# Layer-norm statistics and token sums at other products, a clamp on GpSimd and five denominators on ScalarE, in a linear-attention and ReGLU block

## The chip, the cores and the metric

The kernel runs on one core of one Trainium2 chip. The metric is the time of one execution in microseconds (us); lower is better. Next to each time stands the span, from the first instruction to the last in the core's own records.

The engines: PE is TensorE, DVE VectorE, ACT ScalarE, POOL GpSimd, SP the engine that issues most DMAs.

## The reference

```python
def A(x, wqkv, wo):                        # S = 2048, D = 1024, 32 heads of 32
    q, k, v = split(x @ wqkv)
    phi = lambda t: where(t > 0, t + 1, exp(t)) + 1e-6
    kv, z = sum_s phi(k) v, sum_s phi(k)   # linear attention, not causal
    o = (phi(q) @ kv) / (phi(q) . z + 1e-6)
    return o @ wo
h  = x + A(layernorm(x), wqkv, wo)
h2 = h + ReGLU_FFN(layernorm(h))           # F = 3584; gate * (gate > 0) * up, then W_down
```

## The kernel before

Large products are not done block by block. A *group* forms a 2 by 2 block product from seven smaller products, P1 to P7, of four matmuls each (a fast matrix multiplication). DVE forms sums of the tokens (`x_sums`) and of the weights beforehand; ACT copies PSUM banks between the products (the *fork copies* `fk1`, `fk2`, and `s7`, `sc`), since a later product accumulates on a copy of an earlier one. Other work is hung between the products: `hook(i)` runs its own functions, and those that the group before left in `pend[i]`.

```python
def sgroup(...):                                       # cut to the order of things
    prod(a, X(0,0), W(0,0), True, "P1");  ident_act(bank(b), bank(a), ...)  # fk1, ACT
    hook(1)
    prod(f, SX(2), TW(2), True, "P7");    ident_act(s7, bank(f), ...)
    hook(2)
    prod(b, SX(1), TW(1), False, "P6");   ident_act(bank(c), bank(b), ...)  # fk2, ACT
    hook(3)
    prod(a, X(1,0), W(1,0), False, "P2")  # then e11
    hook(4)
    prod(c, SX(0), TW(0), False, "P5");   ident_act(sc, bank(c), ...)
    hook(5)
    prod(b, X(1,1), TW(3), False, "P4")
    hook(6)
    prod(c, SX(3), W(1,1), False, "P3")
    pend[1] = list(s22[2:]) + s12 + list(s21[1:])      # phi's of this group, in the next
    hook(7)
```

The function phi is an exponential on ACT (`ex`), then on DVE a clamp and a max (`fin`):

```python
def fin():
    PL.add("dve", lambda e: e.tensor_scalar(out=E, in0=E, scalar1=1.0, scalar2=1e-6,
                                            op0=ALU.min, op1=ALU.add), ...)          # clamp
    PL.add("dve", lambda e: e.scalar_tensor_tensor(out=dst_ap, in0=src, scalar=C1, in1=E,
                                                   op0=ALU.add, op1=ALU.max), ...)   # max
```

The order of the work: start-up; groups k0, v2, k1, v3, k2, v4, k3, v5, k4, v6, k5, v7, k6, k7 (kN and vN form the keys and the values of pair N of token tiles, 2N and 2N+1; "P6 of k1" is product P6 of group k1); four query groups for the first half of the tokens and four for the second half; an output stage of 16 token tiles; the FFN. For the token tiles 7, 9, 11, 13 and 15 the first layernorm's statistics are three steps on ACT (a mean, and two halves of the squares, "split"; tiles 5 and 6 have their squares in one piece, the other tiles' statistics are on DVE), then come small operations on GpSimd, and a normalisation on DVE (`norm`). Their results live in slots, `k = len(ln1_a) % 2`.

```python
def v2(sq=sq):                  # hooks of a v group; sq holds tile 7's squares (p == 0), else nothing
    if sq: sq.pop(0)()          # first half of them, behind P7
def v3(p=p, sq=sq):
    if sq: sq.pop(0)()          # second half, behind P6
    if p == 0: x_sums(1); norm(6)
    else: norm(2 * p + 6)
def v5(p=p):
    norm(2 * p + 7)
    m_, q0_, q_ = ln1_stats_act(2 * p + 9, True)
    m_(); q0_(); late_q.append(q_)       # q_ runs at hook 5 of the next k group
...
def a2_div(st):                 # o = num / den, in the second half of the query groups and later
    # dtmp: DVE adds 1e-6 to the denominators (PSUM, 128x32); rden: DVE reciprocal; o: DVE product
    dma_t(..., oT, o, "T3d_%d" % st)     # DMA transpose of o, issued on SP
for t in range(4, 21):          # output stage; NOT = 4
    if t >= 4: a4_mm(t - 4)              # needs the transposed o of that tile
    if t < 16: a2_num(t); a2_div(t)
    if t >= 4: a4_h(t - 4)               # h = x + product (DVE); frees the product's two banks
    if t >= 5: a4_norm(t - 5)            # ACT, then a DMA transpose of the normalised h, on SP (T5d)
```

The instructions of DVE run in the order of the program, and SP issues its DMAs in order (traces in e5 and e6).

## Time and profile before

| | before |
|---|---|
| time, 4 runs beside the change | 723.83 us (723.75 to 724.64) |
| span of the profiled run | 722.1 us, clock 0.999 |
| PE / DVE / ACT / POOL busy | 714.2 / 587.5 / 359.2 / 108.4 us |

The page of the kernel before, its line of busy times:

```profile
PE 714.2 (99%) x4905; PEld 380.4 (53%) x4905; DVE 587.5 (81%) x1024; ACT 359.2 (50%) x623; POOL 108.4 (15%) x177
```

PE looks full, but a busy PE is not a PE that starts matmuls as fast as it can; the Trainium skill says that the busy share of matmuls is no good measure of the distance to the limit ("Perfetto Trace Analysis", Identifying the Most-Contended Engine), and here the fastest kernel at the end of this study and one of the slowest (e15, 723.9 us of span) both show 99%. What can be won is where the start times break their spacing of 0.86 to 0.88 us per product. PE's waits of the kernel before, from 0 to 240 us (after that there is none); the columns are the wait in total, how often, the longest:

```profile
PE ps L766 <- POOL RXH L545: 1.4, 1, 1.4
PE ps L905 <- DVE RXH L834: 1.1, 1, 1.1
PE ps L766 <- DVE RXH L1229: 0.7, 1, 0.7
PE ps L766 <- ACT ps L771: 0.5, 1, 0.5
PE ps L766 <- DVE RWG L984: 0.4, 1, 0.4
```

The first two lie before 7 us, at the start of the program. The last three are the change's targets. Their places in PE's timeline of the kernel before (start, length, engine, line, operation; in brackets the idle time before it and what ended that):

```profile
31.69 1.02 PE L766 MATMUL ps<-RW,RWG 128*128 128x512 f16 x4 [0.41 <-DVE RWG L984]
32.55 1.03 PE L766 MATMUL ps<-RAB 128*128 128x512 bf16 x4
33.63 1.04 PE L766 MATMUL ps<-RW,RWG 128*128 128x512 f16 x4
...
37.84 1.03 PE L766 MATMUL ps<-RC,RWG 128*128 128x512 f16 x4
39.39 1.04 PE L766 MATMUL ps<-RC,RWG 128*128 128x512 f16 x4 [0.53 <-ACT ps L771]
...
175.79 2.98 PE L766 MATMUL ps<-RW,RE 128*128 128x512 bf16 x13 [0.70 <-DVE RXH L1229]
```

31.69 is P6 of v2, which waits for the token sums (L984) and starts 0.57 later than the spacing would have it; 33.63 is its P5, 1.08 after P2 (32.55), so 0.22 late, though no wait is marked; 39.39 is P6 of k1, 1.55 after P7, so 0.69 late, waiting for a fork copy. ACT's timeline shows why that copy was late:

```profile
36.95 1.06 ACT L804 ACTIVATE RXH<-RE 128x1024 bf16<-128x1024 bf16 x1 [1.58 <-DVE RXH L890]
...
38.13 0.63 ACT L804 ACTIVATE RXH<-RE 128x512 bf16<-128x512 bf16 x1
...
38.76 0.58 ACT L771 ACTIVATE ps<-ps 128x512 f32<-128x512 f32 x1
```

ACT stood idle for 1.58 us before the mean of tile 9 (36.95), until the normalisation of tile 6 (L890) had read its slot of statistics; the mean and half of the squares then ran into the time of the fork copy (38.76).

### The profile page before, as it was taken

What the parts mean: (1) busy time and instruction counts of PE and PEld (TensorE: products, weight loads), DVE (VectorE), ACT (ScalarE), POOL (GpSimd) and SP (SyncE); (2) the same over time, 40 slices, a digit from 0 to 9 for tenths busy, and PEclk for the clock granted to TensorE, in tenths of its full rate; (3) what the DMA queues carried; (4) which work ended last, traced back from release to release, by engine and by line L of the source; (5) the groups of instructions that cost most, each with busy time, mean ns of one, the idle gap of its engine ahead of it and who ended that gap; (6) DMA issues with size and microseconds to landing.
All of it is one profiled execution on the core that took longest, in us unless ns stands there. A gap on an engine that the chain in (4) does not pass through costs nothing.

```text
span 722.1 us, 12877 instructions
## 1 busy us (share of the span) xinstructions
PE 714.2 (99%) x4905; PEld 380.4 (53%) x4905; DVE 587.5 (81%) x1024; ACT 359.2 (50%) x623; POOL 108.4 (15%) x177
## 2 busy tenths in 40 slices
PE   8999999999999999999999999999999999999998
PEld 3444444444444444444444558865555545447887
DVE  7878867898775889889988787887889877887984
ACT  4877666764842456677756111035455545423010
POOL 2311100000360103332321001310000000000331
PEclk9999999999999999999999999999999999999999
DMA  9643245023998797999999989993564572037996
GB/s 310 214 98 80 44 126 163 6 30 72 211 221 262 230 282 236 273 302 312 298 273 275 310 251 322 319 208 114 149 172 135 161 250 78 1 102 249 323 315 178
DMA packets 192989, 143.64 MB, mean 199 GB/s; under 512 B 51872, under 2 KB 170400, under 8 KB 192928
## 3 DMA queue, kind: packets, MB, share of 16 engines
q1 hardware_dynamic: 188224, 138.50, 65.3%
q0 software_dynamic: 4032, 3.67, 3.5%
q8 instruction: 38, 0.62, 0.3%
q10 hardware_dynamic: 672, 0.66, 0.3%
q14 instruction: 23, 0.19, 0.1%
HBM read 98.76 MB, written 32.51 MB: 182 GB/s over the span
## 4 chain that ended last, share of the span: by engine, by line
PE 90%; DVE 6%; issue 1%; ACT 1%; POOL 1%; DMA 0%; ACTq 0%; DVEq 0%
PE ps L766 90%; DVE RAB L852 1%; DVE RE L1205 1%; DVE st L780 1%; DVE RX L849 1%; POOL rstd L790 0%; DVE RW L959 0%; DMA RE<-in_A_x_dram 0%; DVE RC L959 0%; DVE RX L1065 0%; ACT RX L845 0%; ACT RXH L804 0%; DVE RXH L834 0%; DVE rden L1203 0%; ACT ps L771 0%
## 5 line engine op out<-in xcount | busy, mean ns | idle before, releaser
L771 ACT ACTIVATE ps<-ps 128x512 f32<-128x512 f32 (+1 forms) x192 | 108.8, 567 | 217.4 <-PE ps L766 207.1
L766 PE MATMUL ps<-RC,RO 128*128 128x512 f16 x616 | 143.0, 369 | 0.0
L766 PE MATMUL ps<-RH,RWG 128*128 128x512 bf16 x448 | 108.1, 379 | 0.0
L766 PEld LDWEIGHTS ps<-RC,RO 128*128 128x128 f16 x616 | 60.3, 98 | 63.5
L766 PE MATMUL ps<-RC,RWG 128*128 128x512 f16 x320 | 76.7, 379 | 0.5 <-ACT ps L771 0.5
L766 PEld LDWEIGHTS ps<-RH,RWG 128*128 128x128 bf16 x448 | 43.8, 98 | 46.9
L1447 DVE TENSOR_TENSOR RAB<-ps,RAB 128x512 bf16<-128x512 f32 x56 | 37.3, 686 | 31.3 <-PE ps L766 31.3
L766 PE MATMUL ps<-RH,RO 128*128 128x512 bf16 (+1 forms) x256 | 61.2, 379 | 0.0
L766 PE MATMUL ps<-RW,RE 128*128 128x512 bf16 x256 | 57.6, 380 | 0.7 <-DVE RXH L1229 0.7
L1647 POOL DMA_DIRECT2D out_dram<-RX x20 | 17.9, 1257 | 263.3 <-DVE RX L1638 221.0
L766 PE MATMUL ps<-RAB 128*128 128x512 bf16 (+2 forms) x270 | 57.1, 351 | 0.1
L766 PE MATMUL ps<-RW,RAB 128*128 128x256 f16 (+3 forms) x362 | 52.9, 301 | 0.0
L766 PEld LDWEIGHTS ps<-RC,RWG 128*128 128x128 bf16 (+1 forms) x320 | 30.1, 98 | 40.1 <-ACT ps L771 6.1
L771 ACT ACTIVATE RE<-ps 128x512 f32<-128x512 f32 (+1 forms) x64 | 31.5, 502 | 37.8 <-PE ps L766 37.8
L766 PEld LDWEIGHTS ps<-RW,RAB 128*128 128x128 f16 (+1 forms) x362 | 35.4, 98 | 14.5
L1638 DVE TENSOR_TENSOR RE<-ps,RE 128x512 f32<-128x512 f32 x44 | 30.2, 687 | 14.3 <-PE ps L766 13.8
L771 ACT ACTIVATE RAB<-ps 128x512 bf16<-128x512 f32 x56 | 33.3, 595 | 16.5 <-PE ps L766 16.2
L1331 DVE TENSOR_TENSOR RO<-RWG 128x1024 f16<-128x1024 bf16 x54 | 36.9, 684 | 4.9 <-DMA RWG<-in_B_W_up_dram 4.9
L766 PEld LDWEIGHTS ps<-RH,RO 128*128 128x128 f16 (+1 forms) x256 | 24.4, 98 | 29.9 <-ACT RX L771 1.5
L1442 ACT ACTIVATE RAB<-RAB 128x1024 bf16<-128x1024 bf16 x28 | 29.5, 1055 | 19.5 <-DVE RAB L1433 19.0
L766 PEld LDWEIGHTS ps<-RW,RE 128*128 128x128 bf16 x256 | 24.0, 98 | 28.7 <-DVE RXH L1229 1.2
L766 PEld LDWEIGHTS ps<-RAB 128*128 128x128 bf16 (+1 forms) x270 | 26.0, 98 | 24.4 <-ACT RAB L908 1.0
(163 smaller groups left out, 1169.6 us busy)
## 6 DMA issues: line engine op xcount, KB each, us to landing
RWG<-in_B_W_gate_dram SPq DMA_DIRECT2D x28, 512.0 KB, 6.2
RWG<-in_B_W_up_dram SPq DMA_DIRECT2D x28, 512.0 KB, 5.2
RW<-l_scr SPq DMA_DIRECT2D x20, 448.0 KB, 5.6
RW<-in_B_W_down_dram SPq DMA_DIRECT2D x14, 512.0 KB, 5.2
t_scr<-RW SPq DMA_DIRECT2D x14, 512.0 KB, 4.9
l_scr<-RX SPq DMA_DIRECT2D x7, 1024.0 KB, 6.5
RE<-l_scr SPq DMA_DIRECT2D x15, 448.0 KB, 4.9
RE<-in_A_x_dram SPq DMA_DIRECT2D x23, 256.0 KB, 3.8
```

Source lines behind the costliest of these rows:

```text
L766: lambda e: e.matmul(out_ap, lhsT, rhs, start=start, stop=stop, skip_group_check=skip),
L771: PL.add("act", lambda e: e.activation(out=dst, in_=src, func=func), reads=reads, writes=writes, name=name)
L780: PL.add("dve", lambda e: e.bn_stats(out=st6[:, k, c * 6:(c + 1) * 6], in_=src_full[:, c * BCH:(c + 1) * BCH]), reads=[src_chunk_bufs[c]], ...
L849: PL.add("dve", lambda e: e.tensor_scalar(out=Et[:, k, :], in0=Et[:, k, :], scalar1=1.0, scalar2=1e-6, op0=ALU.min, op1=ALU.add), reads=[] ...
L852: PL.add("dve", lambda e: e.scalar_tensor_tensor(out=dst_ap, in0=src, scalar=C1, in1=Et[:, k, :], op0=ALU.add, op1=ALU.max), reads=[src_bu ...
L1205: PL.add("dve", lambda e: e.tensor_tensor(out=osb[:, k, :].rearrange("p (g h e) -> p g h e", h=HPG, e=Dh), in0=nv[:, :, :, 0:Dh], in1=rden ...
L1331: PL.add(eng, lambda e: e.tensor_tensor(out=tb(j, u), in0=f0(u), in1=f1(u), op=ALU.subtract), reads=[B_w[i + x] for x in r] + ([B_T[k + x] ...
L1442: PL.add("act", lambda e: e.activation(out=d, in_=d, func=ACTF.Relu), reads=[], writes=db, name=name)
L1447: PL.add("dve", lambda e: e.tensor_tensor(out=d, in0=bank(b), in1=d, op=ALU.mult), reads=[B_bank[b]], writes=[db], name=name)
L1638: PL.add(eng, lambda e: e.tensor_tensor(out=dst, in0=in0, in1=in1, op=op), reads=reads, writes=writes, name=name)
L1647: PL.add("pool", lambda e: e.dma_start(dst, src, accum_op=ALU.add), reads=[bsrc], writes=[B_hscr[st]], slot=sl, name="acc_%d_%d" % (st, dh))
```

## The change

The intent is to take away these waits. (1) A third slot of statistics; tile 7's squares one product later; tile 9's squares both at hook 5 of k1; for tiles 11, 13 and 15 the first half of the squares two products earlier; one difference of weights for v moved from before k0 to k0's hook 6, and the third pair's token sums one hook earlier. (2) In the second half of the query groups one of four clamps runs on GpSimd, and its max one group later at `pend[3]`; the `dtmp` of tiles 0 to 4 runs on ACT. The diff, cut to its core:

```diff
-            k = len(ln1_a) % 2
+            k = len(ln1_a) % 3
@@ sgroup(..., late=False)
-            pend[1] = list(s22[2:]) + s12 + list(s21[1:])
+            tail = list(s21[1:])
+            if late:
+                pend[3] = [tail.pop()]
+            pend[1] = list(s22[2:]) + s12 + tail
@@ q group
-                   add_phi(*dst(1, 0), "q_%d_%d" % (r, ct)),
-                   add_phi(*dst(1, 1), "q_%d_%d" % (r, ct)), "q%d%d" % (r, ct), hooks)
+                   add_phi(*dst(1, 0), "q_%d_%d" % (r, ct), ("dve", "pool")[r]),   # clamp's engine
+                   add_phi(*dst(1, 1), "q_%d_%d" % (r, ct)), "q%d%d" % (r, ct), hooks, late=r == 1)
@@ a2_div
+            if st <= NE:
+                PL.add("act", lambda e: e.activation(out=dv, in_=nv[:, :, :, Dh], func=ACTF.Identity, bias=tiny[:]), ...)
+            else: ...                                  # on DVE, as before
@@ before k0
-        twv.pop(0)()                                   # a difference of weights, DVE 1.2 us
@@ hooks of the k groups
+            def k4():
+                if p == 0: x_sums(2, 0)
             def k5():
+                if p == 0: x_sums(2, 1)
...
+                while p > 0 and late_q: late_q.pop(0)()
             def k6():
+                if p == 0: twv.pop(0)()
@@ hooks of the v groups
-                v2: first squares half;  v3: second half;  p == 0: x_sums(1), norm(6)
+                v3: first squares half;  v4: second half;  p == 0: norm(6), x_sums(1)
-                v5: m_(); q0_(); late_q.append(q_)
+                v5, p == 0: m_(); late_q.extend([q0_, q_])
+                p > 0: q0_() already at v3, the mean at v5   # cut
```

More of the change, by code (lines that the diff above doesn't have):

```diff
@@ L341, in bass_sequential_preLN__linear_attn_block__glu_gated_reglu__prompt_kernel @@
         neghalf = sb("neghalf", [P, 1], f32)
+        tiny = sb("tiny", [P, 1], f32)
         warm = sb("warm", [P, 8], f32)
@@ L346, in bass_sequential_preLN__linear_attn_block__glu_gated_reglu__prompt_kernel @@
         s2 = sb("s2", [P, 2, 5], f32)
-        s1 = sb("s1", [P, 2, 4], f32)
+        s1 = sb("s1", [P, 3, 4], f32)
         dtmp = sb("dtmp", [P, NDT, H], f32)
@@ L427, in bass_sequential_preLN__linear_attn_block__glu_gated_reglu__prompt_kernel @@
         B_s2 = [bufs("s2_%d_" % i, 5) for i in range(2)]
-        B_s1 = [bufs("s1_%d_" % i, 4) for i in range(2)]
+        B_s1 = [bufs("s1_%d_" % i, 4) for i in range(3)]
         B_junk = _Buf("junk")
@@ L464, in bass_sequential_preLN__linear_attn_block__glu_gated_reglu__prompt_kernel @@
         B_neghalf = _Buf("neghalf")
+        B_tiny = _Buf("tiny")
         B_warm = _Buf("warm")
@@ L557, in bass_sequential_preLN__linear_attn_block__glu_gated_reglu__prompt_kernel @@
         PL.add("pool", lambda e: e.memset(warm[:], 0.0), writes=[B_warm], name="warm0")
+        PL.add("pool", lambda e: e.memset(tiny[:], 1e-6), writes=[B_tiny], name="tiny")
         def act_warm():
@@ L838, in bass_sequential_preLN__linear_attn_block__glu_gated_reglu__prompt_kernel, with phi_steps @@
         phi_ctr = [0]
-        def phi_steps(src, src_buf, dst_ap, dst_buf, name):
+        def phi_steps(src, src_buf, dst_ap, dst_buf, name, eng="dve"):
             k = phi_ctr[0] % NPH
@@ L846, in ex, with low, fin @@
                        reads=[src_buf], writes=[B_E[k]], name=name + "_exp")
-            def fin():
-                PL.add("dve", lambda e: e.tensor_scalar(out=Et[:, k, :], in0=Et[:, k, :], scalar1=1.0,
+            def low():
+                PL.add(eng, lambda e: e.tensor_scalar(out=Et[:, k, :], in0=Et[:, k, :], scalar1=1.0,
                                                       scalar2=1e-6, op0=ALU.min, op1=ALU.add),
                        reads=[], writes=[B_E[k]], name=name + "_e2")
+            def fin():
+                if eng == "dve":
+                    low()
                 PL.add("dve", lambda e: e.scalar_tensor_tensor(out=dst_ap, in0=src, scalar=C1, in1=Et[:, k, :],
@@ L854, in fin, with exlow @@
                        reads=[src_buf, B_E[k]], writes=[dst_buf], name=name + "_phi")
-            return ex, fin
+            if eng == "dve":
+                return ex, fin
+            def exlow():
+                ex()
+                low()
+            return exlow, fin
         def phi(*args):
@@ L993, in x_sums, with sgroup @@
             add(3, xb(1, 0), s(1), ALU.subtract, [B_Sx[1][p]] + bx(1, 0))
-        def sgroup(pool, tok_major, X, SX, W, TW, e11, e12, e21, e22, name, hooks=(), isphi=True):
+        def sgroup(pool, tok_major, X, SX, W, TW, e11, e12, e21, e22, name, hooks=(), isphi=True, late=False):
             hooks = dict(hooks)
@@ L1060, in flush, with add_phi @@
             pend.clear()
-        def add_phi(dst, dst_buf, name):
+        def add_phi(dst, dst_buf, name, eng="dve"):
             def go(p_, pb, s_, sb_):
@@ L1066, in add @@
                            writes=[sb_], name=name + "_add")
-                return (add,) + phi_steps(s_, sb_, dst, dst_buf, name)
+                return (add,) + phi_steps(s_, sb_, dst, dst_buf, name, eng)
             return go
@@ L1199, in a2_div @@
             nv = ps[:, 0:HPG, 0:NG * NUW].rearrange("p h (g w) -> p g h w", w=NUW)
-            PL.add("dve", lambda e: e.tensor_scalar(
-                out=dtmp[:, kd, :].rearrange("p (g h) -> p g h", h=HPG), in0=nv[:, :, :, Dh],
-                scalar1=1e-6, scalar2=None, op0=ALU.add), reads=rb, writes=[B_dt[kd]], name="dtmp_%d" % st)
+            dv = dtmp[:, kd, :].rearrange("p (g h) -> p g h", h=HPG)
+            if st <= NE:
+                PL.add("act", lambda e: e.activation(out=dv, in_=nv[:, :, :, Dh], func=ACTF.Identity, bias=tiny[:]),
+                       reads=rb + [B_tiny], writes=[B_dt[kd]], name="dtmp_%d" % st)
+            else:
+                PL.add("dve", lambda e: e.tensor_scalar(out=dv, in0=nv[:, :, :, Dh], scalar1=1e-6, scalar2=None,
+                                                        op0=ALU.add),
+                       reads=rb, writes=[B_dt[kd]], name="dtmp_%d" % st)
             PL.add("dve", lambda e: e.reciprocal(out=rden[:, kd, :], in_=dtmp[:, kd, :]),
@@ L1960, in k1 @@
                     twq.pop(0)()
+            def k4():
+                if p == 0:
+                    x_sums(2, 0)
             def k5():
-                if p + 2 < NP_:
+                if p == 0:
+                    x_sums(2, 1)
+                elif p + 2 < NP_:
                     x_sums(p + 2, 0)
@@ L1968, in k5 @@
                     sq.extend([q0_, q_])
-                elif B < NST:
+                while p > 0 and late_q:
                     late_q.pop(0)()
             def k6():
-                if p + 2 < NP_:
+                if p == 0:
+                    twv.pop(0)()
+                elif p + 2 < NP_:
                     x_sums(p + 2, 1)
-            return {1: k1, 5: k5, 6: k6}, sq
+            return {1: k1, 4: k4, 5: k5, 6: k6}, sq
         def norm(st):
@@ L1998, in bass_sequential_preLN__linear_attn_block__glu_gated_reglu__prompt_kernel, with v3 @@
             if p + 2 < NP_:
-                def v2(sq=sq):
-                    if sq:
-                        sq.pop(0)()
-                def v3(p=p, sq=sq):
+                late = []
+                def v3(p=p, sq=sq, late=late):
                     if sq:
@@ L2006, in v3, with v4, v5 @@
                     if p == 0:
+                        norm(6)
                         x_sums(1)
-                        norm(6)
                     else:
                         norm(2 * p + 6)
-                def v5(p=p):
+                        if 2 * p + 9 < NST:
+                            m_, q0_, q_ = ln1_stats_act(2 * p + 9, True)
+                            q0_()
+                            late += [m_, q_]
+                def v4(sq=sq):
+                    if sq:
+                        sq.pop(0)()
+                def v5(p=p, late=late):
                     norm(2 * p + 7)
-                    B = 2 * p + 9
-                    if B < NST:
-                        m_, q0_, q_ = ln1_stats_act(B, True)
-                        m_()
-                        q0_()
-                        late_q.append(q_)
+                    if p == 0:
+                        m_, q0_, q_ = ln1_stats_act(9, True)
+                        m_()
+                        late_q.extend([q0_, q_])
+                    elif late:
+                        late[0]()
+                        late_q.append(late[1])
                 def v6(p=p, nq=nq):
@@ L2024, in v6 @@
                         twq.pop(0)()
-                v_group(p + 2, {2: v2, 3: v3, 5: v5, 6: v6})
+                v_group(p + 2, {3: v3, 4: v4, 5: v5, 6: v6})
         assert not twq and not twv and not twk
```

## The prediction

> **What bounds the kernel.** TensorE: the page gives PE 714.2 of 722.1 us busy. Matmul busy time is a poor measure of the distance to the limit (the Trainium skill, "Perfetto Trace Analysis", Identifying the Most-Contended Engine), so I took the spacing of matmul starts from the timeline: a product of four 128x512 matmuls starts every 0.86 to 0.88 us nearly everywhere, at a granted clock of 1.00. Only breaks of this spacing can be won. PE's waits and the timeline show, after the start-up, which the change leaves alone:
> - 31.69 (first v group, P6): 0.57 us over the spacing, for DVE's token sums;
> - 33.63 (same group, P5): 0.22, ACT's second fork copy was late, behind a squares half;
> - 39.39 (second k group, P6): 0.69, ACT's first fork copy started at 38.76, its product had ended at 38.0; ACT was at statistics (mean 36.95, squares 38.13);
> - 175.79 (third output product): 0.77, its banks are freed by h_0 on DVE, busy without a pause since about 163.
> Sum 2.25 us, 0.3%. No such wait stands in later k/v groups or the rest of the query part; after 176 PE keeps its spacing.
>
> **What the change does.**
> 1. It moves one weight difference (DVE 1.22 us, at 27.07) from before the first k group's evictions to its hook 6, and pair 2's token sums one product earlier. The sums end about 1.2 us earlier: the 0.57 goes.
> 2. The squares come one product later, behind the second fork copy: the 0.22 goes.
> 3. A third statistics slot frees the mean of tile 9 from the normalisation of tile 6 (36.29 to 36.84, just before it); ACT was idle from 35.4. Its squares move to the next k group. The 0.69 goes. There two squares halves (0.61 each in ACT's spacing) now stand in one product; the next first fork copy had no slack (ended 45.48, P6 at 45.51), so I give back 0.1.
> 4. In the second half of the query groups, one of four clamps (DVE 0.28) goes to GpSimd, its max one group later, and five denominators (DVE 0.18 each) to ACT. DVE has about 6.7 us of work per 6.53 us group; with 0.5 less it keeps up. But denominator 3 now stands on ACT behind the last exponential, which waits for the last product (ended 167.46): the reciprocal can't start before about 168.4, as before (168.39). From there to h_0's end (7.27 us) only one clamp and denominator 4 leave: of the 0.77 about 0.5 goes.
> GpSimd does a two-input 128x512 in 1.15 us here; I estimate the one-input clamp at no more. Its reader has 1.7. GpSimd shares SBUF interfaces with VectorE (the Trainium skill, "GPSIMD Engine Reference", Specifications), which could lengthen some DVE operations by little.
>
> **Sum.** -0.57 -0.22 -0.69 +0.1 -0.5 = -1.9: 723.8 to 721.9 us, -0.26%. Range 721.1 to 723.3. Faster by over 2%: 0.5%; within 2%: 99%; slower: 0.5%.
>
> **What would show it.** PE's waits have no entries near 31, 33 and 38; near 44 perhaps one of 0.1; near 174, 0.2 to 0.3 remain. DVE busy falls by about 2 us, ACT rises by 1 to 1.5, POOL by about 4. The time from the fifth output product to the end is unchanged within 0.2.
>
> **What would make it wrong.** ACT too full in the second k group; the moved weight difference delays the phi operations and with them pair 1's sums, which the second k group needs (slack about 0.7 by my count); ACT's strided read of PSUM slower than 0.3; the clamp late, so that DVE stands in order behind it; start-up scatter of up to 0.9 us, as the runs before show (723.75 to 724.64), half of the effect.

## The result, and the profile after

| | before | after |
|---|---|---|
| time, 4 runs each of the same rounds | 723.83 us (723.75 to 724.64) | 724.31 us (723.42 to 724.74) |
| span of the profiled run | 722.1 us, clock 0.999 | 722.3 us, clock 1.0 |

The ratio is 1.0002, with a 95% interval of 0.9985 to 1.0020: the same. The predicted 721.9 is missed, and its range (721.1 to 723.3) does not hold the measured time.

The page after, busy times, and PE's waits from 0 to 240 us:

```profile
PE 711.7 (99%) x4849; PEld 380.4 (53%) x4905; DVE 585.6 (81%) x1015; ACT 359.1 (50%) x628; POOL 118.8 (16%) x182
```

```profile
PE ps L769 <- POOL RXH L547: 1.4, 1, 1.4
PE ps L769 <- issue: 1.1, 7, 0.2
PE ps L769 <- DVE RXH L1250: 0.6, 1, 0.6
PE ps L769 <- ACT ps L774: 0.5, 1, 0.5
PE ps L918 <- DVE RXH L837: 0.3, 1, 0.3
```

(56 matmul records are missing in the trace of after, 4849 against 4905; the weight loads are complete. Each hole reads as a wait for "issue", so those seven are no waits.) DVE fell by 1.9 us, as predicted. The two waits of the key and value groups are off the list; one for a fork copy (ACT ps) is new, at another place, and the wait for h_0 (0.7) has become 0.6, not 0.2 to 0.3. PE's timeline after, at the places shown of before:

```profile
30.82 2.02 PE L769 MATMUL ps<-RW,RWG 128*128 128x512 f16 x8
32.89 0.81 PE L769 MATMUL ps<-RAB 128*128 128x512 bf16 x3
33.65 1.04 PE L769 MATMUL ps<-RW,RWG 128*128 128x512 f16 x4
...
37.98 1.93 PE L769 MATMUL ps<-RC,RWG 128*128 128x512 f16 x8
...
175.97 2.76 PE L769 MATMUL ps<-RW,RE 128*128 128x512 bf16 x11 [0.59 <-DVE RXH L1250]
```

P7 and P6 of v2 are now one piece of eight matmuls, and so are those of k1: the waits are gone, as predicted. And yet P5 of v2 starts at 33.65, where it started at 33.63 before. The waits went, and PE arrived no earlier.

To see where the time goes I cut both traces at landmarks: starts of weight loads on PE (complete in all traces) and of fork copies on ACT. Two traces of the same kernel give the same lengths within 0.02 us for most pieces, so 0.1 us can be read here, which a total time does not allow. ("First transposes" are PE's first of the normalised tokens, at 6.66 us in the trace of before. The whole span is these pieces, plus 6.3 to 6.8 us before the first transposes, 9.9 in e17, plus 3.9 after the last weight load.)

| piece, us | before | after | difference |
|---|---|---|---|
| first transposes to P6 of k0 | 18.34 | 19.03 | +0.69 |
| P6 of k0 to P6 of v2 | 6.66 | 6.21 | -0.45 |
| P6 of v2 to its P5 | 1.97 | 1.85 | -0.12 |
| P5 of v2 to P6 of k1 | 5.76 | 5.22 | -0.54 |
| to fk2 of k1 | 1.08 | 1.14 | +0.06 |
| to fk2 of v7 | 58.30 | 58.55 | +0.25 |
| to fk1 of k6 | 5.09 | 5.37 | +0.28 |
| to fk2 of the 2nd query group, second half | 46.74 | 46.74 | 0.00 |
| to the output product of tile 1 | 20.55 | 20.77 | +0.22 |
| to that of tile 2 | 4.63 | 4.53 | -0.10 |
| tile 2 to 8; 8 to 10; 10 to the FFN | 23.18; 7.73; 19.91 | 23.18; 7.74; 19.91 | +0.01 |
| FFN to its last weight load | 491.57 | 491.56 | -0.01 |

So 1.11 us of waits are gone, 0.69 came in before them and 0.71 behind them (the time before the first transposes was 0.11 shorter after; together this is the 0.2 between the spans). Three questions follow. Is the +0.69 of the start-up the change's doing or scatter? What are +0.25 and +0.28? Why did the query part lose 0.22 and win only 0.10?

ACT's timeline gives the mechanism of the first. Before, and then after, the mean of tile 6 in the start-up:

```profile
20.43 1.07 ACT L804 ACTIVATE RXH<-RE 128x1024 bf16<-128x1024 bf16 x1
```

```profile
21.40 1.06 ACT L807 ACTIVATE RXH<-RE 128x1024 bf16<-128x1024 bf16 x1 [0.98 <-DMA RE<-in_A_x_dram]
```

After, ACT stood idle 0.98 us until the load of that tile had landed; everything behind the mean in ACT's order, k0's first fork copy too, came later. The change touches neither this load nor the order of ACT up to there.

### The profile page after: what moved, and what is told of

Read it like the earlier page. It is cut to its first block, busy times and chain, and to the rows that moved or that the text cites. A ratio compares the mean times of both kernels' runs of the same rounds, so it can differ in the third digit from the quotient of the medians.

```text
span 722.3 us, 12827 instructions
## 1 busy us (share of the span) xinstructions
PE 711.7 (99%) x4849; PEld 380.4 (53%) x4905; DVE 585.6 (81%) x1015; ACT 359.1 (50%) x628; POOL 118.8 (16%) x182
## 4 chain that ended last, share of the span: by engine, by line
PE 93%; DVE 2%; DMA 1%; SPq 1%; issue 1%; ACT 1%; DVEq 0%; ACTq 0%
PE ps L769 93%; DMA RE<-in_A_x_dram 1%; SPq L567 1%; DVE RWG L997 0%; ACT RXH L807 0%; DVE RE L859 0%; DVE RX L1081 0%; DVE RX L852 0%; ACT RE L961 0%; DVE RE L1659 0%; DVE RAB L859 0%; DVE RE L1226 0%; ACT RX L848 0%; DVE RXH L1250 0%; DVE RW L972 0%
## 5 line engine op out<-in xcount | busy, mean ns | idle before, releaser
L769 PE MATMUL ps<-RH,RO 128*128 128x512 bf16 (+1 forms) x228 | 55.2, 379 | 1.5
L1463 ACT ACTIVATE RAB<-RAB 128x1024 bf16<-128x1024 bf16 x28 | 29.5, 1055 | 19.5 <-DVE RAB L1454 18.9
```

The lines of the kernel that those rows point to most:

```text
L769: lambda e: e.matmul(out_ap, lhsT, rhs, start=start, stop=stop, skip_group_check=skip),
L1463: PL.add("act", lambda e: e.activation(out=d, in_=d, func=ACTF.Relu), reads=[], writes=db, name=name)
```

## The experiments

The theory that I began with: the added start-up is scatter; the change's waits in the key and value groups are truly gone, but part of this gain exists only if the start-up is early, since other chains fix when v2 and k1 can go on; the query part loses what it wins because the clamp on GpSimd is slow. Rivals: the change itself delays the start-up; GpSimd slows DVE through a shared interface; the denominators on ACT are what holds DVE up. Seventeen experiments ran, and all gave a correct result.

### e1_before_again and e2_after_again: both kernels once more

No edit to either. 

> The kernel before, unchanged, to see the scatter of time and trace. Theory 'scatter': the 0.7 us stall of the first key group (first fork copy late, because ACT waits for the load of x tile 6) in the trace of after is chance at start-up and can show here too; times spread over 723.4 to 724.8. Rival 'caused by the change': this trace has no such stall, as the first one had none. In both, the four waits at 31.7, 33.6, 39.4 and 175.8 stand as before, 2.2 us in sum.

> The changed kernel, unchanged. 'Scatter': the 0.7 us stall of the first key group near 25 us is absent or of another size, and where it is absent the time is about 723.3. 'Caused by the change': it is there again at 0.6 to 0.7 us. In both, GpSimd's clamp takes 1.9 us and VectorE stands 0.5 to 1 us behind it in three groups.

Measured on one chip, 5 runs each: before 723.84 us, after 724.06, each at a ratio of 1.0002 (0.9989 to 1.0014) to the pooled runs of before (723.86). In spans: 722.1 (722.0 to 722.2) and 722.3 (722.2 to 722.7). The trace of the kernel before now has the late start-up, 19.02 us for 18.34, without any change of code. The start-up is scatter: 16 of the 19 traces have 18.9 to 19.7, two (before, and e12 below) have 18.3, e15 20.4. PE's timeline of e1:

```profile
30.70 1.93 PE L766 MATMUL ps<-RW,RWG 128*128 128x512 f16 x8
...
33.71 1.04 PE L766 MATMUL ps<-RW,RWG 128*128 128x512 f16 x4 [0.22 <-ACT ps L771]
...
39.22 1.04 PE L766 MATMUL ps<-RC,RWG 128*128 128x512 f16 x4 [0.28 <-ACT ps L771]
```

The wait at P6 of v2 is not there *in the kernel before*: P7 and P6 are one piece of eight. Its three pieces are 6.13, 2.12 and 5.51 us, for 6.66, 1.97 and 5.76 in the trace that I predicted from. PE, coming 0.68 later out of the start-up, is only 0.05 later at P6 of k1 (both counted from the first transposes). Of the three waits (predicted 0.57 + 0.22 + 0.69), the start-up that is usual here leaves 13.76 us in those three pieces where the changed kernel needs 13.28: 0.48 us to win, not 1.48. The reason stands in the same traces: counted from the first transposes, the token sum that P6 of v2 needs starts on DVE at 24.46 us in the trace of before and at 24.51 in e1, and the fork copy that P6 of k1 needs starts on ACT at 32.10 and 32.15. These chains do not move with PE. All six traces with the kernel before's order in these groups and the usual start-up (e1, e4, e6, e11, e16, e17) have 6.13 to 6.15 and 2.12.

### e3_kv_only and e4_q_only: each half alone

e3 is the changed kernel with the query part put back; e4 has the query part alone.

```diff
 e3:  -  add_phi(..., ("dve", "pool")[r]), ..., late=r == 1        +  as before
      -  if st <= NE:                                              +  if st < 0:
 e4:  all hunks of the key and value groups and the third slot taken back
```

> The key/value part of the change alone. My theory: it gains about 1 us net (waits of 0.57, 0.22, 0.69 go; about 0.5 comes as new small waits), so without the start-up stall about 722.8; the wait at 175.8 stays at 0.77. Rival: the reordering gives back everything it takes, 723.8.

> The query part of the change alone (clamp on GpSimd, late max, denominators on ACT). My theory: the clamp of 1.9 us leaves VectorE no earlier at h_0, the wait at 175.8 falls by 0.1 only, two new waits of 0.1 to 0.15 arise near 155.8 and 162.5: 723.9, no gain. Rival (my prediction): 0.5 us faster, 723.3.

Measured: e3 723.96 us, ratio 0.9998 (0.9984 to 1.0011); e4 724.09, ratio 1.0001 (0.9989 to 1.0014). The times tell nothing apart, and e3's expected 722.8 is missed; the pieces do. e3 has the changed kernel's lengths up to k6 (6.21, 1.86, 5.23, 1.14, 58.57, 5.37) and before's after that (20.56, 4.63). e4 has before's up to k6 (6.13, 2.12, 5.51, 1.08, 58.32, 5.09) and the changed kernel's after (20.77, 4.53). So +0.25 and +0.28 belong to the key and value half, +0.22 and -0.10 to the query half, and the halves do not disturb each other.

### e5_clamp_dve: the clamp back on DVE

```diff
-                   add_phi(*dst(1, 0), "q_%d_%d" % (r, ct), ("dve", "pool")[r]),
-                   add_phi(*dst(1, 1), ...), ..., hooks, late=r == 1)
+                   add_phi(*dst(1, 0), "q_%d_%d" % (r, ct)),
+                   add_phi(*dst(1, 1), ...), ..., hooks)
```

> The change with the clamp back on VectorE in its old order; the denominators stay on ACT. Theory 'clamp': the new waits near 155.8 and 162.5 (0.11 and 0.09 us) go, because VectorE no longer stands behind a 1.9 us clamp; the wait for h_0 is below 0.77 by the denominators that VectorE lost, 0.2. Rival 'denominators on ACT': the two waits stay at 0.1 each.

Measured: 723.87 us beside 723.84 of before, ratio 0.9999 (0.9987 to 1.0012); span in the profile 721.9. The piece up to tile 1 is 20.56, as before, and the wait for h_0 falls by 0.26 (4.37 for 4.63) with the denominators on ACT alone. So the clamp is what costs, and the denominators help by themselves. DVE and GpSimd after, one of three such places:

```profile
150.14 1.22 DVE L1226 TENSOR_TENSOR RE<-ps,rden 128x1024 bf16<-128x1024 f32 x1
152.28 0.69 DVE L859 SCALAR_TENSOR_TENSOR RAB<-RX 128x512 bf16<-128x512 f32 x1 [0.92 <-POOL RX L852]
```

```profile
150.29 1.96 POOL L852 TENSOR_SCALAR RX<-RX 128x512 bf16<-128x512 bf16 x1 [66.58 <-ACT RX L848]
```

The clamp takes 1.93 us on GpSimd in the mean (1920 to 1955 ns), where I had taken a two-input operation's 1.15 for an upper bound. It starts at 150.29, and its max on DVE, at `pend[3]`, waits 0.92 us for it. In the whole query part DVE waits three times for GpSimd, 1.4 us in all. The Trainium skill says that DVE and GpSimd are strictly first in, first out ("Perfetto Trace Analysis", Tensor Engine Instruction); for DVE this trace agrees: the next clamp on DVE, which needs nothing of GpSimd, comes only at 152.89, behind that max.

### e10_clamp_later and e9_clamp_min: a later reader, a shorter clamp

```diff
 e10:  -                pend[3] = [tail.pop()]
       +                pend[5] = [tail.pop()]
 e9, on GpSimd only:
       -   scalar2=1e-6, op0=ALU.min, op1=ALU.add
       +   scalar2=None, op0=ALU.min          # leaves out 1e-6 on purpose; still correct within tolerance
```

> The changed kernel, the max that reads GpSimd's clamp two products later still (1.7 us). Theory 'order': the clamp costs only because VectorE stands in order behind it; then the waits near 155.8 and 162.5 go (0.2 us) although the clamp still takes 1.9, and the wait for h_0 is as with the clamp on VectorE or smaller (0.5 or less). Rival 'contention': VectorE's operations beside the clamp are longer and the waits stay.

> The changed kernel, GpSimd's clamp reduced to the one operation min (without the +1e-6; the result moves by less than a bf16 step). If the 1.93 us are two passes of arithmetic, the clamp falls to about 1.0 to 1.2 and VectorE no longer stands behind it (waits near 155.8 and 162.5 go). If the time is per element whatever the operation (or sharing with VectorE), it stays at 1.8 to 1.95.

Measured: e10 723.39 us (723.16 to 723.57, 4 runs) beside 723.87, ratio 0.9992 (0.9977 to 1.0006); spans 721.6 (721.4 to 721.8) beside 722.1 (721.9 to 722.8, 11 runs). The interval holds 1, so the time alone shows no gain. In the trace the pieces are 20.56 and 4.03: nothing is lost before tile 1, and of the wait for h_0 (0.77, see e6) 0.60 is gone. The prediction had said "about 0.5". The same place, on DVE and on GpSimd:

```profile
152.02 0.29 DVE L852 TENSOR_SCALAR RX<-RX 128x512 bf16<-128x512 bf16 x1 [0.75 <-ACT RX L848]
...
153.56 0.68 DVE L859 SCALAR_TENSOR_TENSOR RAB<-RX 128x512 bf16<-128x512 f32 x1
```

```profile
150.21 1.96 POOL L852 TENSOR_SCALAR RX<-RX 128x512 bf16<-128x512 bf16 x1 [66.58 <-ACT RX L848]
```

The clamp is as long as it was; its reader, now at 153.56, finds it ready, and DVE waits for ACT's exponential instead, which it can afford. In e9 (one run, 723.96 us, its trace alone is used) the clamp with one arithmetic step takes 1.50 us, more than the 1.0 to 1.2 that I had expected of one step; DVE waits once for it (0.5), and the pieces are 20.56 and 4.46. So before tile 1 one wait of 0.5 is absorbed; the three of after, 1.4 together with a longest of 0.9, are not. e9 wins less at h_0 than e10 (4.46 against 4.03), and its trace shows something that may be part of the reason. DVE and GpSimd of e9:

```profile
170.11 0.67 DVE L853 TENSOR_SCALAR RX<-RX 128x512 bf16<-128x512 bf16 x1
```

```profile
169.15 1.48 POOL L853 TENSOR_SCALAR RX<-RX 128x512 bf16<-128x512 bf16 x1 [4.18 <-ACT RX L848]
```

This clamp on DVE, ahead of h_0, takes 0.67 us for 0.28, and its end (170.78) lies just behind that of GpSimd's (170.63).

### e17_quiet: the same operations on GpSimd with DVE idle

Three operations of 128x512 bf16 on GpSimd at the very start, when DVE has nothing to do (its first operation is at 3.58 us): the clamp, a minimum alone, and a subtraction with two inputs. Added to the kernel before:

```diff
+        PL.add("pool", lambda e: e.tensor_scalar(out=E0, in0=E0, scalar1=1.0, scalar2=1e-6, op0=ALU.min, op1=ALU.add), ...)
+        PL.add("pool", lambda e: e.tensor_scalar(out=E1, in0=E1, scalar1=1.0, scalar2=None, op0=ALU.min), ...)
+        PL.add("pool", lambda e: e.tensor_tensor(out=E0, in0=E0, in1=E1, op=ALU.subtract), ...)
```

> The kernel before with three more GpSimd operations of 128x512 bf16 at the very start on unused memory: the two-operation clamp, a clamp of one operation, a two-input subtraction. (They delay the start by about 5 us; the total time is of no interest.) Theory 'arithmetic': 1.9, 1.5 and 1.15 us as in the loaded stretches. Rival 'shared interfaces': the clamp falls well below 1.9 (1.2 or less) where VectorE does nothing.

GpSimd's timeline of e17:

```profile
2.31 1.94 POOL L547 TENSOR_SCALAR RX<-RX 128x512 bf16<-128x512 bf16 x1
4.33 1.51 POOL L549 TENSOR_SCALAR RX<-RX 128x512 bf16<-128x512 bf16 x1
5.92 1.15 POOL L551 TENSOR_TENSOR RX<-RX 128x512 bf16<-128x512 bf16 x1
```

The first ended at 4.25 us and so ran mostly beside an idle DVE, and it takes what it takes beside a busy one (1.94 and 1.93). As the cause of the long clamp the shared interface falls: the clamp is slow by itself, and its second arithmetic step costs 0.43. Nor did it slow DVE in the changed kernel: what DVE runs beside the four clamps of after, products read from PSUM (1.22) and clamps (0.28), is as long as before. But DVE does get slower beside GpSimd in other places: the one clamp of e9 above (0.67 for 0.28), and, at about 682 us in the traces of before and after alike, a two-input `tensor_tensor` of 128x1792 beside one of GpSimd (1.83 for 1.09). Why some are longer and others not was not looked into. (The Trainium skill warns that moving work between these two might not help, because they share a read port: "Perfetto Trace Analysis", Optimizing Scalar/DVE Operations. In the changed kernel it did not help, but not for this reason.)

### e15_warm2: one more instruction on ACT

The +0.28 before k6 has an odd look. ACT's timeline after:

```profile
103.93 0.58 ACT L774 ACTIVATE ps<-ps 128x512 f32<-128x512 f32 x1 [3.01 <-PE ps L769]
```

Here ACT has nothing else to do; the fork copy starts 0.35 us after the last event that it can wait for, where a fork copy otherwise starts 0.07 after it. All seven traces with the changed order up to k6 show it, and none of the seven with before's order. In e15 a second copy of the warm-up exponential stands at the program's start:

```diff
         act_warm()
+        act_warm()
```

> The changed kernel with one more tiny activation at ACT's start. Theory 'place in the program': the late fork copy near 103.9 (0.35 us after the last update that it waited for, otherwise 0.07) is gone or stands at another instruction. Rival 'schedule': it stays at the same fork copy with the same 0.28.

Measured (one run; span 723.9 with a start-up of 20.44): the piece before k6 is 5.09, and the other pieces of these groups are as after (6.21, 1.85, 5.23, 1.14, 58.57). The same fork copy in e15:

```profile
104.89 0.58 ACT L774 ACTIVATE ps<-ps 128x512 f32<-128x512 f32 x1 [2.73 <-PE ps L769]
```

It starts 0.07 after its last event. After has one more such start, at 290.35 us (0.36); e15 has none there, but one at 184.66 (0.38), at an instruction that starts 0.08 after its last event in after. So the late starts have moved to another instruction, as the theory 'place in the program' has it, and no lack of ACT's time makes them. This is one run, whose start-up is also 1.4 us later than after's; what makes the late starts stays open.

### e16_slot3: the third slot alone

```diff
-        s1 = sb("s1", [P, 2, 4], f32)             # and its buffers
+        s1 = sb("s1", [P, 3, 4], f32)
-            k = len(ln1_a) % 2
+            k = len(ln1_a) % 3
```

> The kernel before with the third statistics slot alone. If the mean of tile 9 waited for the normalisation of tile 6 because of the slot, the first fork copy of the second key group starts at its product's end and the wait there (0.44 in a typical start) goes: from P5 of the first v group to P6 of the second key group 5.1 to 5.2 us instead of 5.51. If the mean waits for something else (its tile's load), 5.5 stays.

Measured (one run, span 722.3; its time of 725.98 is the span plus 3.7): P5 of v2 to P6 of k1 takes 5.10 us, for 5.51 in e1. ACT's and PE's timelines of e16:

```profile
36.07 1.05 ACT L804 ACTIVATE RXH<-RE 128x1024 bf16<-128x1024 bf16 x1
...
37.24 0.63 ACT L804 ACTIVATE RXH<-RE 128x512 bf16<-128x512 bf16 x1
```

```profile
38.65 1.93 PE L766 MATMUL ps<-RC,RWG 128*128 128x512 f16 x8
```

The mean of tile 9 no longer stands behind the normalisation of tile 6, it starts 0.80 us earlier than in e1 (both counted from the first transposes), its squares end before the fork copy is due, and P7 and P6 of k1 are one piece of eight. The slot by itself gives 0.41 of the 0.48 us that the whole change of these groups gives in the usual start-up. The rest of that change nets 0.07: P5 of v2 comes 0.27 earlier (1.85 for 2.12), the squares now being behind the second fork copy; but P6 of v2 comes 0.08 later (6.21 for 6.13), and P6 of k1 is 0.12 later than with the slot alone (5.22 for 5.10). In the trace of after the first k pair's last max on DVE ends about 35.9 us, later than before (34.8), behind the moved difference of weights, and half of the weight loads of the products with v (kv) wait 0.17 us for it; I take this for the cause of the 0.12, but no run tested it alone.

### e7_kv_start: free ACT for v2

The changed kernel without its query part, and the squares of tile 6, which stand before k0, split and moved to hooks 1 and 3 of k0, so that a late load holds up ACT less.

```diff
-        m6, q6 = ln1_stats_act(6)
+        m6, q60, q61 = ln1_stats_act(6, True)
-        q6()                                # before v_piece(2, 1)
+                if p == 0: q60()            # k0, hook 1
+                if p == 0: q61()            # k0, hook 3
```

> The key/value part of the change, with the squares of tile 6 in two halves inside the first key group instead of ahead of its first fork copy. If ACT's statistics of tile 6, late because its load lands at about 21, cause the 0.4 to 0.6 us wait near 25, that wait goes, and PE is 0.5 earlier at the second key group than with the key/value part alone; if the load is what PE waits for in another way, it stays. Time: 0.5 below the key/value part if nothing later takes it back.

Measured: 723.63 us (723.41 to 724.2), ratio 0.9998 (0.9984 to 1.0012). The start-up is 18.97 against 19.03 of e3, and P6 of k0 to P6 of v2 takes 6.50 for 6.21: the squares, now between k0's fork copies, cost more than their old place did, though the total shows neither. A miss; e8, with the same split, has the same 6.50.

### e6_defer and e11_defer_t: the wait for h_0 by another way

DVE's clamp and max of the last query group stand before h_0 though nothing needs them so early. e6 is the kernel *before* with them put behind h_0:

```diff
-            pend[1] = list(s22[2:]) + s12 + list(s21[1:])
+            tail = list(s21[1:])
+            if late:                        # the last query group of all
+                pend["last"] = tail         # exp issued at the end of the groups
+                tail = []
+            pend[1] = list(s22[2:]) + s12 + tail
...
                 a4_h(t - LAG)
+                while q_last: q_last.pop()()
```

> The kernel before, only the last query group's last clamp and max are put behind h_0 on VectorE (0.92 us of its queue). If the wait at 175.8 is VectorE's backlog alone, it falls from 0.77 to at most 0.1. Theory 'gain passes': the time falls by 0.7, 723.1. Rival 'later limit': the third to twelfth output products then wait for the transposes of o, which landed only 0.1 to 0.6 us ahead of their product in earlier traces, and by 229 us the gain is mostly gone: 723.6 to 723.8.

Measured: 723.71 us (722.98 to 723.79), ratio 0.9996 (0.9983 to 1.0009); spans 722.0 (721.2 to 722.1). In the trace the wait for h_0 is wholly gone (3.86 for 4.63), without GpSimd. PE's timeline of e6 there and at output tile 9, where it has got a new wait:

```profile
175.18 2.98 PE L766 MATMUL ps<-RW,RE 128*128 128x512 bf16 x12
...
202.61 1.67 PE L766 MATMUL ps<-RW,RE 128*128 128x512 bf16 x7 [0.31 <-DMA RE<-RE]
```

This takes back a part (7.87 for 7.73 in the pieces; 8.04 in e1, so it comes and goes without the change too). The median span shows 0.1 of the 0.77; the profiled run, with a start-up of 19.40, shows 0.5, and where the other runs lost the rest was not traced. The output product needs the DMA transpose of o. In e6 tile 9's o was ready at 192.80 us, but its transpose was issued at 197.43 and landed at 202.25: SP issues in order, and in between it issued a load of weights, the transpose of tile 8's o, a store, and the transpose of a normalised h, which needs ACT's result. e11 is e6 with each transpose of the normalised h issued two tiles later.

```diff
-                a4_norm(t - LAG - 1)
+                t5_q.append((t + 2, a4_norm(t - LAG - 1)))   # returns its DMA transpose, to be issued later
+            while t5_q and t5_q[0][0] <= t: t5_q.pop(0)[1]()
```

> The kernel before with the last max behind h_0 (the gain of 0.77 at 175.8 that was seen) and, in addition, the transposes of the normalised h put two tiles later in the queue that also issues the transposes of o. Theory 'later limit': the transposes of o are held up there; now they are issued within 1 us of their o instead of 3 to 5, land 2 us or more ahead of their products, and the whole 0.77 stays to the end: span about 721.4, 723.1 us in time. Rival: they land as late as before (DMA engines full), nothing changes against the version without this edit.

Measured: 726.68 us (724.75 to 727.91), ratio 1.0034 (1.0020 to 1.0047). The wait is freed (tile 9's o ready at 192.68, issued 194.85, landed 197.94) and the piece is 7.73, but the last piece before the FFN takes 22.12 for 19.91: slower, which neither the theory nor the rival had. PE's timeline and then DVE's:

```profile
222.89 7.08 PE L766 MATMUL ps<-RW,RE 128*128 128x512 bf16 x31 [2.04 <-DVE RXH L1237]
```

```profile
220.48 1.22 DVE L1317 TENSOR_TENSOR RC<-RH 128x2048 f16<-128x2048 bf16 x1 [3.31 <-DMA RH<-RXH]
221.62 1.22 DVE L1237 TENSOR_TENSOR RXH<-ps,RE 128x1024 bf16<-128x1024 f32 x1
```

DVE's sums for the FFN (L1317) wait 3.31 us for the last of the late transposes, and h (L1237), which frees PE's banks, stands behind them on DVE. The same pattern as that of the clamp: a slow producer was moved, and a reader in an ordered queue held up work that did not need it.

### e8_best, e12_best2, e13_best3 and e14_repair: putting parts together

All four start from the changed kernel and put tile 9's first squares half back beside its mean (v5). e8 adds e7's split, e6's order and two kv products one hook later, with the clamp on DVE. e12 is e5 with the squares put back, e6's order, and e11's transposes, two tiles late. e13 is e12 with them one tile late. e14 is e10 with the squares put back and nothing else.

```diff
 all:  -                        late_q.extend([q0_, q_])
       +                        q0_()
       +                        late_q.extend([q_])
 e13:  -                t5_q.append((t + 2, a4_norm(t - LAG - 1)))
       +                t5_q.append((t + 1, a4_norm(t - LAG - 1)))
```

> All repairs together: key/value part without the second squares half in the second key group, the first two tiles' kv accumulation after P3, tile 6's squares split, the last max behind h_0, clamp and denominators on VectorE. Sum of the waits removed against the kernel before: about 2 us at 179 us. Theory 'gain passes': 721.8 to 722.2. Rival 'later limit' (transposes of o, in order on one queue): the output stage gives half or more of it back, 722.8 to 723.4.

> The parts of the change that held (statistics slot, order of squares and sums, denominators on ACT; the squares of tile 9 split over two groups as before), the last max behind h_0, and the transposes of h later. Against the kernel before: 0.5 in the first groups, 0.77 at h_0, nothing given back at the transposes: about 1.2 us, 722.6. If the start-up decides (a wait of 0.5 to 0.6 behind a late load in nearly all traces), single runs scatter by that.

> As the last combined version, with the transposes of the normalised h one tile later instead of two. If those transposes, two tiles late, held up the sums of the FFN's inputs on VectorE and by that h (2 us lost between 214 and 227 us), one tile later loses nothing there, and the transposes of o still land 1 us ahead of their products: PE at the FFN 1.2 to 1.8 us earlier than the kernel before in the same start-up, time about 722.5. Rival: the loss stays at 1 us or more.

> The change with two repairs only: GpSimd's clamp has its reader two products later, and the first squares half of tile 9 goes back beside its mean. Gains add: 0.6 at h_0, 0.5 in the first groups, no 0.25 in the second v group; if the transposes of o near 202 us cap it, at most 0.8 to 0.9 of it reaches the FFN: 723.0 to 723.3. If nothing caps it: 722.6.

| | time, us | before, same chip | ratio (95%) | span, us |
|---|---|---|---|---|
| e8 | 723.76 (723.70 to 724.52) | 723.84 | 1.0003 (0.9990 to 1.0015) | 722.0 (722.0 to 722.8) |
| e12 | 725.28 (724.04 to 727.27) | 723.87 | 1.0020 (1.0008 to 1.0031) | 723.6 (722.3 to 725.5) |
| e13 | 722.65 (722.38 to 722.81) | 724.07 | 0.9978 (0.9965 to 0.9990) | 720.9 (720.7 to 721.1) |
| e14 | 722.84 (722.69 to 723.02) | 724.07 | 0.9981 (0.9968 to 0.9995) | 721.1 (721.0 to 721.3) |

e8 is a miss: its profiled run loses 0.83 us at tiles 8 to 10 (8.56; PE waits 0.99 before the output product of tile 9, whose transpose of o landed at 202.99: the late transposes again), 0.36 from P5 of v2 to P6 of k1 (5.59; with the kv products moved away, P3 of v2 waits 0.31 for an ACT copy), and 0.34 in the FFN, which was not looked into. e12 repeats e11's loss (21.86 before the FFN); by chance it also has an early start-up (18.26), and then the changed order does most of what was predicted (1.08 of 1.48): its next three pieces are 13.31 us, for 14.39 in the equally early trace of before. e13 has all it was made for. PE's waits of e13 from 0 to 240 us:

```profile
PE ps L769 <- POOL RXH L547: 1.4, 1, 1.4
PE ps L918 <- DVE RXH L837: 0.9, 1, 0.9
PE ps L769 <- ACT ps L774: 0.4, 1, 0.4
```

Of these only the last lies behind 7 us: it is at 25.35, P6 of k0, the end of the start-up. The output stage has none: transposes one tile late land at 196.04 for tile 9, 5.4 us before its product, and the FFN is reached in 19.91. In pieces, e13 against the kernel before with an equal start-up:

| piece, us | e1 (before) | after | e13 |
|---|---|---|---|
| first transposes to P6 of k0 | 19.02 | 19.03 | 18.99 |
| to P6 of k1, three pieces | 13.76 | 13.28 | 13.29 |
| to fk2 of k1 | 1.08 | 1.14 | 1.08 |
| to fk2 of v7 | 58.30 | 58.55 | 58.40 |
| to fk1 of k6 | 5.09 | 5.37 | 5.09 |
| to fk2 of the 2nd query group, second half | 46.74 | 46.74 | 46.74 |
| to the output products of tiles 1; 2 | 20.56; 4.63 | 20.77; 4.53 | 20.56; 3.86 |
| tile 8 to 10 | 8.04 | 7.74 | 7.73 |

The squares of tile 9, both at k1's hook 5, cost 0.15 of the +0.25 and the 0.06 before it; with one half put back (e8, e12, e13, e14) the piece to v7 is 58.40 to 58.42. What makes the remaining 0.10 was not looked for. With one half put back the late start before k6 is gone too. e14 shows that the change needed two small repairs: with them it wins 0.19%, and its interval excludes 1. That is 1.2 us between the medians, of the predicted 1.9; in the traces 0.3 of it (and of e13's gain) lies at tiles 8 to 10, where before itself scatters (7.73 and 8.04).

## Why the prediction was wrong

Predicted -1.9 us; measured nothing, within the interval. Term by term:

1. **The step that failed first: "-0.57 -0.22 -0.69".** The waits were read rightly, and the change removes them (13.28 us in the three pieces after, 14.39 before). But they were summed as time to be won, from one trace whose start-up was 0.7 us earlier than is usual. In the kernel before with its usual start-up (e1) the same pieces take 13.76 us: the first wait does not exist there, because the chain on DVE that fixes P6 of v2 has not moved (24.46 and 24.51 us behind the first transposes) and PE comes to meet it. So 0.48 us was to be won, and 1.08 (predicted 1.48) only after an early start-up (e12 against the first trace of before). The prediction named start-up scatter as noise on the result; it did not see that the waits absorb it, so that each belongs to one start-up only.
2. **"I give back 0.1" for the two squares halves in k1.** The sign and place were right; the size was 0.21 (0.06 and 0.15, from putting one back), and with it stand 0.10 that is not explained and 0.28 of a late start on ACT that nothing in the dependences explains, present in seven of seven traces of this order.
3. **"I estimate the one-input clamp at no more" than 1.15 us, and "Its reader has 1.7".** This step failed outright: 1.93 us, and the room was 1.07 us at the first place and 1.73 at the next two; DVE stood behind it for up to 0.9 us, and 0.21 was lost before the output stage. "Of the 0.77 about 0.5 goes" therefore became 0.10. The rest of that step was right: with the reader two products later (e10) the gain is 0.60, with the denominators alone (e5) 0.26. "The clamp late, so that DVE stands in order behind it" was in the list of what would make it wrong. The shared interface, which I named as a small risk, did not make the clamp long (e17: 1.94 against 1.93) nor DVE slower beside it in this kernel; in e9 one clamp on DVE beside it did take 0.67 for 0.28.
4. **Smaller ones.** DVE's busy time fell by 1.9 (predicted about 2). ACT's was to rise by 1 to 1.5 and went from 359.2 to 359.1, though the five denominators are there, at 0.28 us each (DVE waited 0.8 us once for the one that stands behind the last exponential, as expected); the durations of ACT's records, each counted in full, do rise by 1.3 (383.6 to 384.9), but in the busy time overlapping records count once, and that sum did not. POOL rose by 10.4, not 4: the clamps make 7.7 of it. Within the first 40 us, POOL's busy time is 2.4 larger, of which a second trace of before has 2.0 by itself. The time from the FFN's start is unchanged (491.57 and 491.56), as predicted.

In the usual start-up the schedule of the change sums to -0.48 + 0.06 + 0.25 + 0.28 + 0.21 - 0.10 = +0.22 us (columns e1 and after above; the transposes at tiles 8 to 10 left out, which scatter in both). The measured +0.2 of e2's median span agrees. That the terms that ate the gain can be removed, all but 0.10 of the 0.25, is shown, each by runs that have it no more: the clamp's (e5, e10), the squares' and the late start's (e8, e12, e13, e14). The causes of the 0.10 and of ACT's late start are open.

## What to carry to other kernels

Take two or three traces of the kernel before adding up its small waits: a wait that another chain sets absorbs whatever PE gains ahead of it, so its length in one trace is not time to be won. When work is moved to another engine, take that operation's duration on that engine from a trace, and give its reader more room than that, because in an ordered queue a late reader holds up everything behind it. Cut the traces at landmarks and compare the pieces: effects of 0.2 us that cancel in the total time are plain there, and a change that "does nothing" may hold a gain that two small repairs set free.

## What the Trainium skill lacked or had wrong

- "GPSIMD Engine Reference", 4.1 Engine selection, says of elementwise work on GpSimd that two-input operations are about two times slower than on VectorE and that "1-input is roughly line-rate". Here a one-input `tensor_scalar` of 128x512 bf16 takes 1.93 us with two arithmetic steps and 1.50 with one, against 1.15 for a two-input subtraction on the same engine and 0.28 for the same clamp on VectorE. One input is slower than two, by 1.3 to 1.7 times.
- "GPSIMD Engine Reference", 3.1 Elementwise — side-by-side cycle accounting, gives about 2.6 cycles per element for a two-input `tensor_tensor`; with the 1.2 GHz of the page's own example I estimate 1.11 us for 512 elements, and 1.15 was measured, so this agrees. It gives 1.03 cycles per element for "k ≤ 2" without saying in that section what k is; the same estimate, 0.44 us, is far from both one-input operations here (1.50 and 1.93). The section's table has no one-input `tensor_scalar`, and no cost of its second arithmetic step (0.43 us here).
- "TensorE: Matmul & The Clock Gate", Back-to-back issue gap, gives about 131 ns per matmul of N=512 as sustained in a stream of weight loads and matmuls. Here such a stream runs four in 0.86 us, 216 ns each, at a clock of 1.00; this is the page's formula for an isolated matmul.
- None of the pages that I read has the late starts of ACT: 0.35 us after the last event, instead of 0.07, at one place of the program in seven traces of seven, gone, with another elsewhere, in the one run with one more instruction before it (e15).
